# Half of a held store moved ahead of the last loads: 48 of its 128 partitions in eight transfers of 6

## The chip, the cores and the metric

The kernel runs on one core of one Trainium2 chip. The metric is the device time in microseconds of one execution: the median of 3 runs before the change is 260.25 us.

## What is computed

Attention over channels with normalised columns, then a mixture of depths in which 128 tokens of each batch pass through a small network and replace their rows. There are four batches of 6208 tokens with 256 channels, in float32.

```python
qn = q / (np.linalg.norm(q, axis=1, keepdims=True) + 1e-06)
kn = k / (np.linalg.norm(k, axis=1, keepdims=True) + 1e-06)
s = kn.transpose(0, 2, 1) @ qn / tau
a = softmax(s)                      # 256 x 256 per batch
x = v @ a                           # 6208 x 256 per batch
...
scores = np.einsum('bsd,d->bs', x, w_gate)
out = x.copy()
for b in range(B):
    top_idx = np.argpartition(-scores[b], capacity)[:capacity]
    xe = x[b, top_idx]
    ye = np.maximum(xe @ w1, 0.0) @ w2
    g = 1.0 / (1.0 + np.exp(-scores[b, top_idx]))
    out[b, top_idx] = x[b, top_idx] + g[:, None] * ye
```

## The kernel before

A batch is cut into units: six chunks of 1024 rows (128 partitions by 8 rows of 256 channels) and a remainder of 64 rows. GpSimd issues all loads, cast from float32 to bfloat16 on the way; `units` lists them batch by batch, first the q and k chunks, then the v chunks, in the order chunk 0, remainder, chunks 1 to 5. The last chunk of q and k and the last chunk of v of the last batch are loaded in two halves of four rows (`pieces`, L229).

TensorE first sums k times q over the rows of a batch. A softmax chain follows (`softmax_stages`), then the transposes of v (`p2_transpose`), the gate scores (`p2_score`) and the output products (`p2_out`), whose PSUM results ScalarE or VectorE copies into one of nine staging tiles `stage` of 128 x 8 x 256 float32 (1 MB). One staging tile is one store, issued by SyncE (`emit_store`, L671; the remainder L673). When all scores of a batch exist, `select_stages` searches the threshold of the 128 highest scores in seven steps (cmp L715, counts m_ps L735), finds the tokens (tri_b L765, oh L786), gathers their v rows (L803), transposes them (L827), runs the network and scatters the 128 updated rows (L908).

The queues are in order, and the program's order is written by a planner that runs while the kernel is built: `Engines` and `Rings` keep an estimate of each engine's and of the transfers' time, and the main loop at the end picks the piece of work whose estimated data are there. `Rings.landing` estimates when a transfer lands; `Rings.fetch` adds 1.2 us for each fetch of code to one of eight lags in turn, and a landing waits for the largest lag. Where TensorE would wait in the late phase, the planner puts in matmuls whose result nobody reads (`unread`, L593).

Stores of the last two batches, and the last two of the batch before them, are held back while loads run (`back`, `deferred`): the first of them waits for a gate (`GATE`, L230), the landing of the first half of the very last v unit, and the others stand behind it in SyncE's queue. That queue, the gate and the estimates that follow from them (`stage_ready`, `out_store`) are what the change touches.

Of the kernel before, what the change touches and what calls it, by code (L numbers as in the profile page):

```python
# [17 lines left out]
P = 128  # L18
# [11 lines left out]
class Rings:  # L30
# [9 lines left out]
        self.lag[self.fetched % 8] += FETCH  # L40
        self.fetched += 1

    def add(self, ring, ready, dur, key, tail):
        self.q[ring].append((ready, dur, key, tail))

    def run(self, until):
        while True:
            heads = [r for r in (0, 1) if self.q[r]]
            if not heads:
                return  # L50
            nxt = max(self.t, min(self.q[r][0][0] for r in heads))
            if nxt > until:
                return
            self.lag = [max(0.0, x - (nxt - self.t)) for x in self.lag]
            self.t = nxt
            able = [r for r in heads if self.q[r][0][0] <= nxt]
            r = able[0] if len(able) == 1 else 1 - self.last
            ready, dur, key, tail = self.q[r].pop(0)
            self.last = r
            self.t = nxt + dur  # L60
            self.done[key] = self.t + tail + max(self.lag)

    def landing(self, key):
        if key in self.done:
# [60 lines left out]
def kernel(  # L125
# [12 lines left out]
    nc = tc.nc  # L138
# [52 lines left out]
    def view(t, b, ci):  # L191
        if ci < NFULL:
            return lview(t, b, ci // CPL)[:, ci % CPL * RPP:(ci % CPL + 1) * RPP, :]
        return lview(t, b, NL)
# [15 lines left out]
    def late(b, ci):  # L210
        return b == E and ci in LATE

    def back(b, ci):
        return b >= E or b == E - 1 and ci in BACK

    LOAD = 2.445
    STORE = 2.45
    rings = Rings()
    eng = Engines()
# [5 lines left out]
    units = []  # L225
    for b in range(B):
        units += [("qk", b, d) for d in lorder] + [("v", b, d) for d in lorder]
    if LR == 8:
        pieces = {("qk", L, LAST): (4, 4), ("v", L, LAST): (4, 4)}  # L229
        GATE = ("v", 0) + units[-1]  # L230
    else:
        pieces = {("qk", 0, FIRST): (8, 8), ("qk", L, LAST): (8, 4, 4), ("v", L, LAST): (8, 4, 4)}
        GATE = ("v", 8) + units[-1]
    loaded = {}
    pair_of = {}
    load_inst = {}
# [127 lines left out]
    stage_of = {}  # L364
# [621 lines left out]
    def stage_ready():  # L986
# [4 lines left out]
            return stage_free[key]  # L991
        return rings.landing(("st",) + key)

    def out_store(b, ci):
        dep = stage_done[(b, ci)]
        if back(b, ci) and not gate_done:
            dep = max(dep, rings.landing(GATE))
        if late(b, ci):
            dep = max(dep, rings.landing(("scatter", E)))
        parts = (2 if b == L else 1) if ci < NFULL else 1  # L1000
        for h in range(parts):
            key = ("st", b, ci) if h == parts - 1 else ("st", b, ci, h)
            issued = eng.issue("sp", 0.42, dep)
            rings.add(1, issued + 0.65, STORE / parts + 0.009 if ci < NFULL else 0.2, key, 0.45)
            ins = emit_store(b, ci, h, parts)
        stored[b].append(key)
        if not late(b, ci):
            held[b] -= 1
        return ins

    while True:
# [17 lines left out]
        if deferred and GATE in load_inst and (held[E] == 0 or any(b == E for b, _ in deferred)):  # L1029
            for b, ci in [d for d in deferred if d[0] == E] or list(deferred):  # L1030
                deferred.remove((b, ci))
                st = out_store(b, ci)
                if not gate_done:
                    gate_done.append(1)
                    tc.add_manual_dep(
                        st.ins, load_inst[GATE].ins.name,
                        mybir.DependencyInfo(mybir.DependencyClass.Sync, mybir.DependencyReason.DATA),
                        reason="stores behind the last loads")
        t = now()
        able = []  # L1040
        for c in chains:
# [145 lines left out]
```

## Time and profile before

| | us |
|---|---|
| median of 3 runs | 260.25 |
| lowest and highest run | 258.79, 260.44 |
| the profiled execution, its own time | 259.43 |
| its span, first to last instruction | 257.4 |
| busy in the span: PE | 206.8 (80%) |
| DVE, ACT | 104.3 (41%), 99.4 (39%) |
| HBM read and written | 78.91 MB, 25.95 MB |

Times within the program count from the span's start. PE is TensorE, DVE is VectorE, ACT is ScalarE, POOL is GpSimd, SP is SyncE; SPq is SyncE's queue of transfers. DMA share is the mean busy share of the core's sixteen transfer engines, and GB/s is what they wrote, so a load counts with its bfloat16 bytes. A row of the timeline gives start, duration, engine, line, operation, output and inputs, count, and in brackets the idle time before it with what ended it.

### The profile page before, as it was taken

The page shows a single profiled execution, that of the slowest core. Times are in us where ns is not written, and L with a number is a line of the kernel's source. Part 1 is how long each engine was busy: PE and PEld are TensorE (multiplying, and loading weights), DVE is VectorE, ACT ScalarE, POOL GpSimd, SP SyncE. Part 2 cuts the span into 40 slices and gives each one's busy share as a digit, 9 for nine tenths or more (in the row PEclk, how much of TensorE's full clock was granted, in tenths as well). Part 3 has the DMA queues.
Part 4 walks back from the last instruction along what each step waited for, and adds up shares of the span by engine and source line. Part 5 has one row for each costly group of instructions (what it writes and reads, how often), then busy time and mean ns, then how long its engine had stood idle before and what let it go on. Part 6 is the DMA issues. An engine that isn't in the chain of part 4 may idle for free.

```text
span 257.4 us, 6080 instructions
## 1 busy us (share of the span) xinstructions
PE 206.8 (80%) x2585; PEld 171.4 (67%) x2585; DVE 104.3 (41%) x414; ACT 99.4 (39%) x182; POOL 56.2 (22%) x105
## 2 busy tenths in 40 slices
PE   0099697788888969999998759689998989887980
PEld 0068476676767849997676549577776879665860
DVE  0200002657552263436660011656657266676230
ACT  2800003630000587763943001660233298364750
POOL 8223223123204230100034123213214200001301
PEclk9999889799999997999999799999999999999998
DMA  6999999999999999999999999999999997999995
GB/s 236 259 218 213 213 213 211 215 212 213 213 214 212 214 259 288 279 333 313 315 291 333 308 221 211 214 212 214 211 215 212 212 211 185 402 425 414 401 419 233
DMA packets 16844, 66.84 MB, mean 260 GB/s; under 512 B 2097, under 2 KB 3634, under 8 KB 13618
## 3 DMA queue, kind: packets, MB, share of 16 engines
q0 software_dynamic: 12528, 38.93, 75.8%
q1 hardware_dynamic: 4290, 27.53, 26.4%
q8 instruction: 20, 0.33, 0.5%
q14 instruction: 6, 0.05, 0.0%
HBM read 78.91 MB, written 25.95 MB: 407 GB/s over the span
## 4 chain that ended last, share of the span: by engine, by line
DMA 54%; PE 24%; issue 8%; ACT 4%; DVE 4%; POOL 2%; POOLq 1%; SPq 0%; ACTq 0%
DMA qk_ch<-in_k_dram 29%; DMA qk_ch<-in_q_dram 13%; DMA v_ch<-in_v_dram 12%; PE o_ps L641 8%; PE s_ps L426 4%; PE g_ps L430 4%; ACT stage L659 2%; PE vt_ps L558 2%; PE m_ps L735 1%; PE sc_ps L607 1%; POOL qk_ch L261 1%; ACT vt_sb L576 1%; DVE qk_ch L579 1%; DVE cmp L715 1%; PE g_ps L641 1%
## 5 line engine op out<-in xcount | busy, mean ns | idle before, releaser
L426 PE MATMUL s_ps<-qk_ch 128*128 128x256 bf16 x288 | 68.8, 284 | 21.4 <-DMA qk_ch<-in_k_dram 21.4
L430 PE MATMUL g_ps<-qk_ch 128*128 128x256 bf16 x288 | 68.6, 284 | 0.0
L659 ACT COPY stage<-o_ps 128x512 f32<-128x512 f32 x79 | 44.7, 590 | 40.0 <-PE o_ps L641 38.0
L426 PEld LDWEIGHTS <-qk_ch 128*128 128x128 bf16 x288 | 29.3, 102 | 28.3 <-DMA qk_ch<-in_k_dram 23.3
L641 PE MATMUL o_ps<-a_sb,vt_sb 128*128 128x256 bf16 (+1 forms) x278 | 40.2, 274 | 3.1 <-ACT stage L659 2.1
L641 PEld LDWEIGHTS <-vt_sb 128*128 128x128 bf16 (+1 forms) x294 | 27.5, 98 | 9.9 <-issue 6.0
L430 PEld LDWEIGHTS <-qk_ch 128*128 128x128 bf16 x288 | 29.3, 102 | 4.5
L558 PEld LDWEIGHTS <-v_ch 128*128 128x128 bf16 x384 | 24.5, 101 | 4.2 <-issue 3.5
L558 PE MATMUL vt_ps<-ident_b,v_ch 128*128 128x128 bf16 x328 | 24.9, 226 | 2.9 <-ACT vt_sb L576 2.9
L261 POOL DMA_DIRECT2D qk_ch<-in_q_dram x25 | 13.8, 552 | 44.4 <-PE vt_ps L558 8.7
L261 POOL DMA_DIRECT2D v_ch<-in_v_dram x25 | 13.5, 551 | 29.3 <-DMA qk_ch<-in_q_dram 18.2
L466 DVE SCALAR_TENSOR_TENSOR junk<-g_ps,ident_f 128x128 f32<-128x128 f32 x6 | 1.7, 292 | 44.6 <-ACT e L457 44.5
L261 POOL DMA_DIRECT2D qk_ch<-in_k_dram x25 | 13.6, 545 | 26.7 <-DMA v_ch<-in_v_dram 15.3
L739 DVE TENSOR_REDUCE cnt<-m_ps 128x8 f32<-128x392 f32 (+2 forms) x28 | 12.0, 429 | 16.3 <-PE m_ps L735 15.9
L579 DVE COPY vt_sb<-vt_ps 128x1024 bf16<-128x1024 bf16 x20 | 13.5, 689 | 12.0 <-PE vt_ps L558 12.0
L715 DVE SCALAR_TENSOR_TENSOR cmp<-sc,wl,tab 128x392 bf16<-128x392 f32 x28 | 17.5, 627 | 1.0
L908 POOL DMA_INDIRECT out_dram<-upd,idx x4 | 4.0, 991 | 62.8 <-DMA out_dram<-stage 31.3
L576 ACT COPY vt_sb<-vt_ps 128x1024 bf16<-128x1024 bf16 (+1 forms) x19 | 16.3, 906 | 1.2 <-PE vt_ps L558 1.0
L457 ACT COPY e<-g_ps 128x256 f32<-128x256 f32 x3 | 1.1, 372 | 31.5 <-PE g_ps L430 31.5
L607 PE MATMUL sc_ps<-aw_sb,vt_sb 128*128 128x2 bf16 (+1 forms) x294 | 11.1, 164 | 1.5 <-DVE sc L683 0.6
L441 PE MATMUL s_ps<-qk_ch 128*128 128x256 bf16 x96 | 11.9, 273 | 0.0
L607 PEld LDWEIGHTS <-vt_sb 128*128 128x128 bf16 (+1 forms) x294 | 10.1, 96 | 2.7 <-DVE vt_sb L579 1.6
(180 smaller groups left out, 268.7 us busy)
## 6 DMA issues: line engine op xcount, KB each, us to landing
out_dram<-stage SPq DMA_DIRECT2D x18, 1024.0 KB, 14.3
qk_ch<-in_q_dram POOLq DMA_DIRECT2D x23, 512.0 KB, 14.6
qk_ch<-in_k_dram POOLq DMA_DIRECT2D x23, 512.0 KB, 18.9
v_ch<-in_v_dram POOLq DMA_DIRECT2D x23, 512.0 KB, 16.9
out_dram<-stage SPq DMA_DIRECT2D x12, 512.0 KB, 8.2
stage<-in_moe_w_dram SPq DMA_DIRECT2D x2, 1024.0 KB, 5.0
qk_ch<-in_q_dram POOLq DMA_DIRECT2D x2, 256.0 KB, 16.0
qk_ch<-in_k_dram POOLq DMA_DIRECT2D x2, 256.0 KB
```

What stands on the lines that cost most here:

```text
L261: ins = nc.gpsimd.dma_start(out=t[:, rows, :], in_=lview(src, b, d)[:, rows, :])
L426: nc.tensor.matmul(s_ps[:, cc, :].rearrange("p (i c) -> p i c", i=2), lhsT=pair[:parts, 1, s, cc * P:(cc + 1) * P], rhs=pair[:parts, :, s, ...
L430: nc.tensor.matmul(g_ps[:, cc, :].rearrange("p (i c) -> p i c", i=2), lhsT=blocks[:parts, at, :], rhs=blocks[:parts, at:at + step + 1:step ...
L441: nc.tensor.matmul(s_ps[:, cc, :], lhsT=kt[:parts, s, cc * P:(cc + 1) * P], rhs=qt[:parts, s, :], start=d == FIRST and s == 0 and cc == 0, ...
L558: nc.tensor.transpose(vt_ps[:, cc, j, :parts], in_=vt[:parts, v0 + j, cc * P:(cc + 1) * P], identity=ident_b[:parts, :parts])
L576: nc.scalar.copy(vt_sb[:, :, :n, :parts], vt_ps[:, :, :n, :parts])
L579: nc.vector.tensor_copy(vt_sb[:, :, :n, :parts], vt_ps[:, :, :n, :parts])
L607: nc.tensor.matmul(sc_ps[:parts, col, :], lhsT=vt_sb[:, cc, j, :parts], rhs=aw_sb[:, cc, :], start=cc == 0 and col == 0, stop=cc == 1 and ...
L641: nc.tensor.matmul(o_ps[:parts, pj, :], lhsT=vt_sb[:, cc, j, :parts], rhs=a_sb[:, cc, :], start=pj == 0 and cc == 0, stop=last and cc == 1 ...
L659: nc.scalar.copy(st[:parts, rows, :], o_ps[:parts, :m, :])
L715: nc.vector.scalar_tensor_tensor(out=cmp, in0=sc[:, :, None].to_broadcast([P, NCOL, NTHR]), scalar=wl[:, i, NTHR:NTHR + 1], in1=tab[:, Non ...
L739: nc.vector.tensor_reduce(out=cnt9[:, 0:NTHR], in_=mps[:, 0:wide * NTHR].rearrange("p (s j) -> p j s", s=wide), axis=AX.X, op=ALU.add)
```

## The change

The first held store is split. Its partitions 0 to 47 go in eight transfers of six partitions each (every fourth partition, from 0 to 3 and from 24 to 27 on); the first of the eight waits for the landing of the v unit that is fifth from the end (`EIGHTS_GATE`, chunk 1 of the last batch) and the other seven follow it in SyncE's queue. Partitions 48 to 127 go in one transfer that waits for `GATE` as the whole store did. The planner's estimates follow: each of the eight counts 0.75 us on SyncE and 0.32 us of transfer, and takes that time off the eight lags of the code fetches.

```diff
--- before.py
+++ after.py
@@ -40,8 +40,8 @@
         self.lag[self.fetched % 8] += FETCH
         self.fetched += 1
 
-    def add(self, ring, ready, dur, key, tail):
-        self.q[ring].append((ready, dur, key, tail))
+    def add(self, ring, ready, dur, key, tail, eight=False):
+        self.q[ring].append((ready, dur, key, tail, eight))
 
     def run(self, until):
         while True:
@@ -55,10 +55,12 @@
             self.t = nxt
             able = [r for r in heads if self.q[r][0][0] <= nxt]
             r = able[0] if len(able) == 1 else 1 - self.last
-            ready, dur, key, tail = self.q[r].pop(0)
+            ready, dur, key, tail, eight = self.q[r].pop(0)
             self.last = r
             self.t = nxt + dur
-            self.done[key] = self.t + tail + max(self.lag)
+            if eight:
+                self.lag = [max(0.0, x - dur) for x in self.lag]
+            self.done[key] = self.t + tail + (0.0 if eight else max(self.lag))
 
     def landing(self, key):
         if key in self.done:
@@ -228,6 +230,7 @@
     if LR == 8:
         pieces = {("qk", L, LAST): (4, 4), ("v", L, LAST): (4, 4)}
         GATE = ("v", 0) + units[-1]
+        EIGHTS_GATE = ("v", 0) + units[-5]
     else:
         pieces = {("qk", 0, FIRST): (8, 8), ("qk", L, LAST): (8, 4, 4), ("v", L, LAST): (8, 4, 4)}
         GATE = ("v", 8) + units[-1]
@@ -991,10 +994,36 @@
             return stage_free[key]
         return rings.landing(("st",) + key)
 
+    def behind(store, key):
+        tc.add_manual_dep(
+            store.ins, load_inst[key].ins.name,
+            mybir.DependencyInfo(mybir.DependencyClass.Sync, mybir.DependencyReason.DATA),
+            reason="stores behind the last loads")
+
     def out_store(b, ci):
         dep = stage_done[(b, ci)]
         if back(b, ci) and not gate_done:
+            st = stage_of[(b, ci)]
+            for i, p0 in enumerate([a + j for a in (0, 24) for j in range(4)]):
+                ps = slice(p0, p0 + 21, 4)
+                ins = nc.sync.dma_start(out=view(out, b, ci)[ps], in_=st[ps])
+                if i == 0:
+                    dep = max(dep, rings.landing(EIGHTS_GATE))
+                    behind(ins, EIGHTS_GATE)
+                issued = eng.issue("sp", 0.75, dep)
+                key = ("st", b, ci, "e", i)
+                rings.add(1, issued + 0.65, 0.32, key, 0.45, True)
+                stored[b].append(key)
             dep = max(dep, rings.landing(GATE))
+            issued = eng.issue("sp", 0.42, dep)
+            key = ("st", b, ci)
+            rings.add(1, issued + 0.65, STORE * 80 / P, key, 0.45)
+            ins = nc.sync.dma_start(out=view(out, b, ci)[48:P], in_=st[48:P])
+            behind(ins, GATE)
+            gate_done.append(1)
+            stored[b].append(key)
+            held[b] -= 1
+            return ins
         if late(b, ci):
             dep = max(dep, rings.landing(("scatter", E)))
         parts = (2 if b == L else 1) if ci < NFULL else 1
@@ -1029,13 +1058,7 @@
         if deferred and GATE in load_inst and (held[E] == 0 or any(b == E for b, _ in deferred)):
             for b, ci in [d for d in deferred if d[0] == E] or list(deferred):
                 deferred.remove((b, ci))
-                st = out_store(b, ci)
-                if not gate_done:
-                    gate_done.append(1)
-                    tc.add_manual_dep(
-                        st.ins, load_inst[GATE].ins.name,
-                        mybir.DependencyInfo(mybir.DependencyClass.Sync, mybir.DependencyReason.DATA),
-                        reason="stores behind the last loads")
+                out_store(b, ci)
         t = now()
         able = []
         for c in chains:
```

SyncE's queue round the first held store (the fourth `128x2048` of its group in before; `stage` is a staging tile, `stage_rem` that of a remainder). Before:

```order
L671 DMA out_dram<-stage 128x2048 x6
L673 DMA out_dram<-stage_rem 64x256
L671 DMA out_dram<-stage 128x2048 x4
L673 DMA out_dram<-stage_rem 64x256
L671 DMA out_dram<-stage 128x2048 x5
L671 DMA out_dram<-stage 64x2048 x2
```

After:

```order
L674 DMA out_dram<-stage 128x2048 x6
L676 DMA out_dram<-stage_rem 64x256
L674 DMA out_dram<-stage 128x2048 x3
L1009 DMA out_dram<-stage 6x2048 x8
L1021 DMA out_dram<-stage 80x2048
L676 DMA out_dram<-stage_rem 64x256
L674 DMA out_dram<-stage 128x2048 x5
L674 DMA out_dram<-stage 64x2048 x2
```

One store of 128 partitions has become eight of 6 and one of 80; all that follows stands in the order that it had.

TensorE's queue where the last v chunk is transposed (L558, L561 in after), behind fillers on `w_sb` and `ident_b`. Before:

```order
L607 MATMUL sc_ps<-aw_sb,qk_ch 128x2
L593 LDWEIGHTS ident_b
L593 MATMUL sc_ps<-w_sb,ident_b 128x256
L593 LDWEIGHTS ident_b
L593 MATMUL sc_ps<-w_sb,ident_b 128x256
L593 LDWEIGHTS ident_b
L593 MATMUL sc_ps<-w_sb,ident_b 128x256
L593 LDWEIGHTS ident_b
L593 MATMUL sc_ps<-w_sb,ident_b 128x256
L558 LDWEIGHTS v_ch
L558 MATMUL vt_ps<-ident_b,v_ch 128x128
```

After:

```order
L561 MATMUL s_ps<-ident_b,v_ch 128x128
L596 LDWEIGHTS ident_b
L596 MATMUL sc_ps<-w_sb,ident_b 128x256
L596 LDWEIGHTS ident_b
L596 MATMUL sc_ps<-w_sb,ident_b 128x256
L596 LDWEIGHTS ident_b
L596 MATMUL sc_ps<-w_sb,ident_b 128x256
L561 LDWEIGHTS v_ch
L561 MATMUL vt_ps<-ident_b,v_ch 128x128
```

Four fillers ahead of these transposes have become three. Behind them four fillers have become two, and the transposes of the chunk's first half have moved from ahead of 32 score matmuls to behind them.

TensorE's queue in the last batch's search, between the counts over partitions (`tri_b`) and the token matmuls (`oh`); each output group is four matmuls from `a_sb`. Before:

```order
L765 MATMUL m_ps<-own_b,tri_b 128x1
L641 LDWEIGHTS qk_ch
L641 MATMUL s_ps<-a_sb,qk_ch 128x256
...
L786 LDWEIGHTS oh
L786 MATMUL m_ps<-wtab,oh 128x50
```

After:

```order
L768 MATMUL m_ps<-own_b,tri_b 128x1
L644 LDWEIGHTS qk_ch
L644 MATMUL o_ps<-a_sb,qk_ch 128x256
...
L644 MATMUL g_ps<-a_sb,qk_ch 128x256
...
L789 LDWEIGHTS oh
L789 MATMUL m_ps<-wtab,oh 128x50
```

One output group (into s_ps) between the two has become two (o_ps and g_ps). Counted from the first output group of the last batch, 17 groups stood ahead of `oh` and 19 do now, so that 7 whole groups behind it have become 5; the 16 groups behind those, which also take the second-last batch's correction, are as they were. ScalarE now copies one staging piece that VectorE copied. GpSimd's queue is the same in both.

## Rows read from the trace of the kernel before

**Rows 1.** The page's slices: DMA share in tenths and GB/s, 40 slices of 6.4 us.
```profile
DMA  6999999999999999999999999999999997999995
GB/s 236 259 218 213 213 213 211 215 212 213 213 214 212 214 259 288 279 333 313 315 291 333 308 221 211 214 212 214 211 215 212 212 211 185 402 425 414 401 419 233
```

**Rows 2.** Windows by stage; the last two columns are DMA share and GB/s.
```profile
207.50:214.00 6.50, 5.59 (x88) 5.10 (x85) 3.96 (x17) 6.50 (x15) 0.00 (x0) 1.00 1.07 211
214.00:218.00 4.00, 3.85 (x78) 3.52 (x76) 2.06 (x7) 2.74 (x7) 0.00 (x0) 1.00 0.54 137
218.00:254.00 36.00, 29.20 (x342) 23.16 (x339) 17.53 (x65) 18.61 (x35) 3.95 (x4) 1.00 1.01 412
254.00:257.40 3.40, 0.00 (x0) 0.00 (x0) 0.00 (x0) 0.00 (x0) 0.00 (x0) 0.72 0.16 65
```

**Rows 3.** Windows of half a microsecond round the last load, the same columns.
```profile
214.50:215.00 0.50, 0.40 (x17) 0.31 (x13) 0.00 (x0) 0.50 (x3) 0.00 (x0) 1.00 0.53 98
215.00:215.50 0.50, 0.44 (x4) 0.31 (x4) 0.00 (x0) 0.50 (x3) 0.00 (x0) 1.00 0.64 115
215.50:216.00 0.50, 0.50 (x7) 0.41 (x6) 0.32 (x2) 0.08 (x1) 0.00 (x0) 1.00 0.61 111
216.00:216.50 0.50, 0.50 (x16) 0.50 (x14) 0.30 (x1) 0.00 (x0) 0.00 (x0) 1.00 0.35 62
216.50:217.00 0.50, 0.50 (x13) 0.50 (x11) 0.50 (x2) 0.16 (x1) 0.00 (x0) 1.00 0.06 12
217.00:217.50 0.50, 0.50 (x13) 0.50 (x11) 0.43 (x3) 0.50 (x1) 0.00 (x0) 1.00 0.05 8
217.50:218.00 0.50, 0.50 (x13) 0.50 (x11) 0.50 (x2) 0.50 (x2) 0.00 (x0) 1.00 1.23 524
```

**Rows 4.** SyncE: wait for the gate; store issues (ns min/median/max); timeline from 216 us.
```profile
SPq L671 <- DMA v_ch<-in_v_dram: 87.5, 1, 87.5
...
L671 SPq DMA_DIRECT2D out_dram<-stage x30: 332/540/1767, 90.1 to 247.8; - x30
...
216.69 0.33 SPq L671 DMA_DIRECT2D out_dram<-stage  x1
...
217.68 9.41 SPq L671 DMA_DIRECT2D out_dram<-stage  x7
```

**Rows 5.** The chain that ended last, from 204 us: start, us, what.
```profile
204.19 13.56 DMA v_ch<-in_v_dram
```

**Rows 6.** TensorE's timeline: last v transposes with fillers (L593), output groups, gathered rows (L827).
```profile
219.93 0.60 PE L593 MATMUL sc_ps<-w_sb,ident_b 128*128 128x256 bf16 x4
220.36 0.61 PE L558 MATMUL vt_ps<-ident_b,v_ch 128*128 128x128 bf16 x8
220.81 0.60 PE L593 MATMUL sc_ps<-w_sb,ident_b 128*128 128x256 bf16 x4
...
238.26 0.60 PE L641 MATMUL s_ps<-a_sb,qk_ch 128*128 128x256 bf16 x4
238.70 0.60 PE L641 MATMUL o_ps<-a_sb,qk_ch 128*128 128x256 bf16 x4
...
246.78 0.38 PE L648 MATMUL o_ps<-d_b,late_oh 128*128 128x256 bf16 x2
247.00 0.28 PE L827 MATMUL vt_ps<-ident_b,vg 128*128 128x128 bf16 x2
```

**Rows 7.** GpSimd's timeline from 236 us.
```profile
238.14 0.99 POOL L803 DMA_INDIRECT vg<-in_v_dram,idx  x1 [1.11 <-DVE idx L797]
...
251.86 0.97 POOL L908 DMA_INDIRECT out_dram<-upd,idx  x1 [7.91 <-DVE upd L894]
```

**Rows 8.** Timeline: copies into the staging tiles that waited for a store.
```profile
238.47 0.69 DVE L656 COPY stage<-o_ps 128x512 f32<-128x512 f32 x1 [0.60 <-DMA out_dram<-stage]
...
241.09 0.59 ACT L659 COPY stage<-s_ps 128x512 f32<-128x512 f32 x1 [0.29 <-DMA out_dram<-stage]
```

**Rows 9.** The page's DMA queues: the one that fetches code (packets, MB, share).
```profile
q8 instruction: 20, 0.33, 0.5%
```

## The prediction

> **What bounds the kernel now.** I read the page's slices first. DMA stands at 9 tenths from the second slice to the last but one, and dips once between, in the slice from 212 to 219 us [rows 1]. So the core is bound by its transfers, and what matters is where their engines run dry. Windows by stage say the same in numbers: a share of 1.07 while the last loads run (shares a little over 1 are overlapping packets), 0.54 for the four microseconds round the landing of the last load, 1.01 for the 36 us of stores, 0.16 in the tail [rows 2]. The hole is worth 4.00 x (1.07 - 0.54) = 2.1 us of all sixteen engines.
>
> Windows of half a microsecond show its shape [rows 3]. From 214.5 to 216.0 the share stands at 0.53 to 0.64, against 1.07 before, then it falls to 0.06: about half of the engines have finished the last loads some 2 us before the other half, and from 216.5 to the restart just before 218 nearly all are idle. The late end of the plateau is the gate. SyncE's wait for the first half of the last v unit lasted 87.5 us, the store behind it was issued at 216.69, and the first store bytes run about 1.2 us later [rows 3, 4]. The last load lands at 204.19 + 13.56 = 217.75 us [rows 5].
>
> After the hole two things run side by side. The store stream is at its full 412 GB/s until 254 [rows 2]. The compute chain of the last batch goes from the last v chunk over the threshold search and the gather (238.14) to the last scatter (251.86) [rows 7]. They are tied together: copies into the staging tiles waited for a store 0.60 us at 238.47 and 0.29 us at 241.09 [rows 8], so the matmuls whose results those copies take are already paced by when stores free tiles.
>
> **What the change does to the transfers.** It takes 48 of 128 rows of 8 KB, 393,216 bytes, out of the first held store. At 412 GB/s [rows 2] these are 0.95 us of all sixteen engines, and everything behind that store in SyncE's queue starts 0.95 us sooner, provided that the 48 rows cost the loads nothing.
>
> When they run: the gate of the eight is the landing of v chunk 1, behind which chunks 2 to 5 remain, 4 x 0.524 MB written at 211 GB/s [rows 2] = 9.9 us. The last load lands at 217.75 with one late engine, most are done by 217, so the eight are released at about 207.5. All loads have been issued by then (the last one at 204.19 [rows 5]), so nothing on GpSimd is moved. On SyncE only work waits behind them that is gated until 216.69 anyway [rows 4].
>
> Issue cost: eight more instructions. The 30 stores of before took 0.33 to 1.77 us each on SyncE, median 0.54 [rows 4]. At the median they take 4.3 us and are issued by 212; the limit is (216.69 - 207.5)/8 = 1.15 us each, above which SyncE would reach the gate late. I take the median: the long ones are in the crowded store phase. Later issues have room: seven in 9.41 us [rows 4], while 1 MB takes 2.55 us to move.
>
> What they cost the loads: nothing in before shows a six-row transfer, so this is bounded from both sides. One 8 KB row on one engine is 2.55/8 = 0.32 us (1 MB is eight such rows on each of sixteen engines). If each transfer puts one row on each of six engines, those six get 8 x 0.32 = 2.55 us more, the others none. If the six belong to the half that is done about 2 us early [rows 3], they finish at 214.5 + 2.55, about 217.05, no later than the other half and ahead of the last landing: cost 0. If they belong to the late half, the gate and the last loads come 2.55 us later. What makes one half late is the fetching of code: 20 packets that take 0.5% of sixteen engines' span [rows 9], 0.005 x 16 x 257.4 / 20 = 1.03 us each; some 17 of them fall before 215 us, and 17.5 us over eight engines are 2.2 us each, the length of the plateau. So eight engines pay for all of the code and eight for none, as the planner's own account in Rings has it, and any six of the second eight cost nothing. I take 0, at four chances in five.
>
> [...]
>
> **What it does to the order.** Two places of TensorE's queue move. The transposes of the last v chunk stand behind three filler matmuls instead of four, and two instead of four follow; in before these stand at 219.93 and 220.81 in front of the transposes and scores that feed the search [rows 6], though the chunk had landed at 217.75. Eight filler matmuls there become five, 3 x 0.11 = 0.33 us, so the search may start 0.3 us or more earlier. And 19 output groups instead of 17 stand ahead of the token matmuls on oh (L786), so two fewer (2 x 0.44 = 0.87 us [rows 6]) stand between these and the transposes of the gathered rows, which ran at 247.00 right behind the last output group [rows 6]. GpSimd's queue is unchanged. None of this can outrun the staging tiles: the copies that waited at 238.47 and 241.09 wait for stores which now land 0.95 us sooner. So the compute chain can come forward by about as much as the stores, and a little less where the gather's own landing is next: PE reached it without a wait worth a row, and it was issued 8.8 us before.
>
> **The sum.** Stores 0.95 us sooner; the scatter 0.33 to 0.95 sooner; both end together, so I take 0.85 us. The profiled execution has a span of 257.4 and took 259.43 us; it becomes 258.6. The median of the runs is 260.25, 0.8 above that execution, so I forecast 260.25 - 0.85 = 259.4 us, 0.3% less. For this kernel about 1% is what a measurement can tell from no change.
>
> **Rivals.**
>
> A, the end is held by the compute chain. From the issue of the last scatter at 251.86 to the end of the span 5.5 us pass whatever the stores do. If the gather lands no sooner (transfers behind a full queue take their turns), only the filler part is gained, 0 to 0.35 us: 260.0 us. For it: DMA is nearly empty in the tail, 0.16 [rows 2]. Against it: the copies' waits for stores [rows 8].
>
> B, the six engines are late ones, or the rows are spread over both halves. Then the gate opens up to 2.55 us later, at 219.2, and the stream of stores gains 0.95 of it back: +1.6 us, 261.85. The last landing, at 217.75 or up to 217.05 + 2.55, costs the transposes little, which stood at 220.36 anyway [rows 6]. It decides from the point at which the extra work on a late engine exceeds 0.95 us, three of eight rows. For it: no row ties the six to the early half. Against: the plateau leaves room on eight engines. [...]
>
> C, SyncE is too slow with them: at 1.77 us each they end at 207.5 + 14.2 = 221.7, the gated store starts 5.0 us late, and all stores behind it: 260.25 + 5.0 - 0.95 = 264.3. For it: the 1.77 exists [rows 4]. Against: with the engines not crowded by stores, an issue took 0.33 [rows 4].
>
> That the eight are not done before the gate, and so change nothing, needs a release after 215; the landing of chunk 1 excludes it.
>
> **Chances.** Forecast 0.60, A 0.19, B 0.15, C 0.06. More than 1% faster would need 2.6 us, more than the 2.1 us of the hole: only the scatter of runs (258.79 to 260.44) could show it, 0.02. More than 1% slower is C, and B where the late landing holds the search as well: 0.08. Within 1%: 0.90. The forecast's own range, gains of 0.4 to 1.2 us, is 259.05 to 259.85; with A at its upper end and the scatter of the runs (1.5 below the median, 0.2 above, and as much again for a median of three), the range is 258.0 to 261.2. B's full price lies outside.
>
> **What would show it.** Right: half-microsecond shares near 1 up to about 216.5 instead of the plateau; the gated store issued at 216.7 within 0.3; the last v load still landing near 217.8; copies into staging, the gather and the last scatter 0.3 to 1 us earlier. Step by step wrong: a gate issue near 219 is B; eight issues that run past 216.7 are C; everything earlier but the last scatter still at about 251.8 is A; an unchanged plateau means the six engines aren't the early ones.

## The result, and the profile after

The median is 261.69 us after the change (9 runs, 261.03 to 262.96), against 259.92 us for the kernel before on the same chip (9 runs, 258.78 to 261.12). The ratio is 1.0067, with a 95% interval of 1.0043 to 1.0090: slower by 1.7 us, not faster by 0.85. The profiled execution has a span of 260.5 us and took 262.44; it lies 0.75 above its median, that of before 0.5 below, so the two profiles stand 3.1 us apart where the medians stand 1.8.

The slices of the page, against [rows 1], show the dip before the stores where it was, and deeper (121 GB/s for 185):

```profile
DMA  6999999999999999999999999999999994999994
GB/s 234 261 216 216 211 213 215 212 213 212 214 213 216 208 264 288 267 318 316 311 303 335 316 216 213 213 211 215 215 210 211 213 222 121 391 423 414 398 424 186
```

SyncE's timeline and its waits, against [rows 4]: the eights were issued from 206.95 on, 0.74 us each, as planned. The gated store (L1021) was issued at 219.28, 2.59 us later than the 216.69 of before, after a second wait for a load of 6.3 us.

```profile
206.95 5.89 SPq L1009 DMA_DIRECT2D out_dram<-stage  x8
219.28 0.34 SPq L1021 DMA_DIRECT2D out_dram<-stage  x1
...
220.34 9.58 SPq L674 DMA_DIRECT2D out_dram<-stage  x7
...
SPq L1009 <- DMA v_ch<-in_v_dram: 76.5, 1, 76.5
...
SPq L1021 <- DMA v_ch<-in_v_dram: 6.3, 1, 6.3
```

Windows of after round the last loads, against [rows 3] (the last two columns are DMA share and GB/s). The plateau of before is filled: 0.92 where it had 0.53. But the share doesn't end there: it falls to 0.17 by 218 and stands at 0.06 to 0.07 from 218 to 220, as it stood at 0.05 to 0.06 from 216.5 to 217.5 in before. One engine of sixteen is 0.0625. So by these shares one engine alone is still loading, and the gated store waits for it. (A window counts a packet, its time and its bytes, where the packet starts, so the share of a short window can pass 1.)

```profile
214.50:215.00 0.50, 0.50 (x20) 0.50 (x18) 0.18 (x1) 0.50 (x2) 0.00 (x0) 1.00 0.92 213
...
216.00:216.50 0.50, 0.34 (x6) 0.26 (x4) 0.00 (x0) 0.50 (x3) 0.00 (x0) 1.00 0.64 152
...
217.50:218.00 0.50, 0.50 (x13) 0.50 (x11) 0.50 (x2) 0.00 (x0) 0.00 (x0) 1.00 0.17 41
218.00:218.50 0.50, 0.50 (x13) 0.50 (x11) 0.47 (x2) 0.49 (x1) 0.00 (x0) 1.00 0.07 12
...
219.50:220.00 0.50, 0.32 (x9) 0.28 (x9) 0.50 (x2) 0.43 (x1) 0.00 (x0) 1.00 0.06 12
```

The trace holds one thing more, which no view prints: the times of the sixteen increments of a load's semaphore, as many as there are engines (for each of the eights, six come as its six rows land). I read each as one engine. Those of the load that is the gate fall in groups. In before, seven come from 213.04 to 213.49, eight from 215.10 to 215.58 and one at 216.63. In after, three come by 213.18, eleven from 215.05 to 215.53, and the last two at 217.46 and 219.26. The early group has lost four of its seven: four of the six engines of the eights were early ones, and two were not.

Windows by stage, of after, against [rows 2]:

```profile
207.50:214.00 6.50, 5.59 (x75) 4.93 (x73) 4.29 (x21) 6.50 (x14) 0.00 (x0) 1.00 1.06 224
214.00:218.00 4.00, 3.84 (x86) 3.50 (x84) 1.64 (x5) 2.75 (x6) 0.00 (x0) 1.00 0.62 141
218.00:220.00 2.00, 1.80 (x41) 1.68 (x38) 1.93 (x5) 1.93 (x2) 0.00 (x0) 1.00 0.07 12
220.00:222.50 2.50, 2.47 (x47) 1.96 (x45) 1.50 (x3) 0.00 (x0) 0.00 (x0) 1.00 0.96 275
222.50:254.00 31.50, 26.00 (x274) 20.28 (x274) 14.54 (x61) 18.31 (x35) 2.98 (x3) 1.00 1.01 415
```

And of before in the same stretches:

```profile
218.00:220.00 2.00, 1.75 (x52) 1.64 (x50) 1.66 (x3) 0.77 (x1) 0.00 (x0) 1.00 0.98 393
220.00:222.50 2.50, 2.15 (x32) 1.75 (x30) 1.02 (x4) 0.00 (x0) 0.00 (x0) 1.00 1.00 380
222.50:254.00 31.50, 25.30 (x264) 19.77 (x262) 14.86 (x58) 17.84 (x34) 3.95 (x4) 1.00 1.02 416
```

Here is the second thing, which the prediction had not thought of. In the first 2.5 us of the restarted stream the engines are as busy as ever (0.96), but write 275 GB/s, where before wrote 393 at 0.98. From 222.5 on the rate is what it was.

The compute chain follows, against [rows 6, 7]: the last transposes of v stand at 221.27 (before 220.36), the gather at 239.79 (238.14), the last scatter at 254.46 (251.86). TensorE's and GpSimd's timelines of after:

```profile
221.27 0.61 PE L561 MATMUL vt_ps<-ident_b,v_ch 128*128 128x128 bf16 x8
...
239.79 0.99 POOL L806 DMA_INDIRECT vg<-in_v_dram,idx  x1 [0.30 <-issue]
...
254.46 0.97 POOL L911 DMA_INDIRECT out_dram<-upd,idx  x1 [7.81 <-issue]
```

This leaves three theories for the late gate and the loss. Late engines (rival B): at least one of the six engines was among the last with its loads, and 8 x 0.32 us came on top. Order: the moved instructions cost it. Late start: the eights run beside the last loads too late, whichever engines they use. The 275 GB/s point to a second cost, called crowding below: the rest of the store moves its rows slowly.

### The profile page after: what moved, and what is told of

The parts are those of the page before. It is cut to its first block, busy times and chain, and to the rows that moved or that the text cites. A ratio compares the mean times of both kernels' runs of the same rounds, so it can differ in the third digit from the quotient of the medians.

```text
span 260.5 us, 6083 instructions
## 1 busy us (share of the span) xinstructions
PE 210.0 (81%) x2581; PEld 174.1 (67%) x2581; DVE 103.9 (40%) x413; ACT 99.8 (38%) x183; POOL 56.2 (22%) x105
## 4 chain that ended last, share of the span: by engine, by line
PE 46%; DMA 27%; ACT 9%; issue 6%; DVE 5%; POOL 2%; POOLq 1%; SPq 0%; DVEq 0%; ACTq 0%
DMA qk_ch<-in_k_dram 11%; PE s_ps L429 8%; PE g_ps L433 8%; PE o_ps L644 7%; DMA out_dram<-stage 7%; DMA vg<-in_v_dram,idx 5%; PE vt_ps L561 5%; DMA v_ch<-in_v_dram 5%; ACT vt_sb L579 4%; PE sc_ps L610 3%; PE s_ps L444 3%; PE g_ps L414 2%; PE m_ps L738 2%; ACT stage L662 2%; ACT e L525 1%
## 5 line engine op out<-in xcount | busy, mean ns | idle before, releaser
L429 PE MATMUL s_ps<-qk_ch 128*128 128x256 bf16 x288 | 70.8, 290 | 16.1 <-DMA qk_ch<-in_k_dram 16.1
L433 PE MATMUL g_ps<-qk_ch 128*128 128x256 bf16 x288 | 70.6, 290 | 0.0
L429 PEld LDWEIGHTS <-qk_ch 128*128 128x128 bf16 x288 | 29.9, 104 | 22.4 <-DMA qk_ch<-in_k_dram 16.7
L433 PEld LDWEIGHTS <-qk_ch 128*128 128x128 bf16 x288 | 30.0, 104 | 5.3 <-issue 0.2
L561 PE MATMUL vt_ps<-ident_b,v_ch 128*128 128x128 bf16 x328 | 26.1, 232 | 3.7 <-ACT vt_sb L579 3.7
L561 PEld LDWEIGHTS <-v_ch 128*128 128x128 bf16 x384 | 25.4, 103 | 4.8 <-issue 3.5
L444 PE MATMUL s_ps<-qk_ch 128*128 128x256 bf16 x96 | 12.0, 273 | 0.0
```

Of the source, the lines that this page charges most:

```text
L429: nc.tensor.matmul(s_ps[:, cc, :].rearrange("p (i c) -> p i c", i=2), lhsT=pair[:parts, 1, s, cc * P:(cc + 1) * P], rhs=pair[:parts, :, s, ...
L433: nc.tensor.matmul(g_ps[:, cc, :].rearrange("p (i c) -> p i c", i=2), lhsT=blocks[:parts, at, :], rhs=blocks[:parts, at:at + step + 1:step ...
L444: nc.tensor.matmul(s_ps[:, cc, :], lhsT=kt[:parts, s, cc * P:(cc + 1) * P], rhs=qt[:parts, s, :], start=d == FIRST and s == 0 and cc == 0, ...
L561: nc.tensor.transpose(vt_ps[:, cc, j, :parts], in_=vt[:parts, v0 + j, cc * P:(cc + 1) * P], identity=ident_b[:parts, :parts])
```

## The experiments

In all of them the same numbers are computed and stored; only the pieces of the first held store, their gate, or the order change. A ratio is to the kernel before on the same chip.

**Order and transfers apart.** e1 has the order of the change and the store of before:

```diff
-                ins = nc.sync.dma_start(out=view(out, b, ci)[ps], in_=st[ps])
...
-            ins = nc.sync.dma_start(out=view(out, b, ci)[48:P], in_=st[48:P])
+            ins = nc.sync.dma_start(out=view(out, b, ci), in_=st)
```

> Instruction order of the changed kernel, transfers of the kernel before (one store of 128 partitions at the gate, nothing earlier). Theory 1 (a late engine: the eight transfers put 2.55 us on at least one transfer engine that is among the last to finish the loads): the gated store is issued near 216.7 us as before, time within 0.4 us of before. Theory 2 (the planner's new order costs the time): about 1.7 us slower than before, gate unchanged.

Measured: 259.74 us, ratio 0.9997 (0.9975 to 1.0020). The gated store stands where it was:

```profile
216.43 0.33 SPq L1019 DMA_DIRECT2D out_dram<-stage  x1
```

The order costs nothing that shows.

e2 has the transfers of the change, and the planner's estimates, so the order, of before:

```diff
-                issued = eng.issue("sp", 0.75, dep)
-                key = ("st", b, ci, "e", i)
-                rings.add(1, issued + 0.65, 0.32, key, 0.45, True)
...
-            rings.add(1, issued + 0.65, STORE * 80 / P, key, 0.45)
+            rings.add(1, issued + 0.65, STORE + 0.009, key, 0.45)
```

> Transfers of the changed kernel (eight of 6 partitions, then 80 at the gate), instruction order of before on all other engines. Theory 1: the gated store is issued near 219.3 us and the time is 1.4 to 2.0 us above before, as with the whole change. Theory 2: gate near 216.7, time the same as before or up to 0.9 us less.

Measured: 261.57 us, ratio 1.0073 (1.0047 to 1.0099). From the first issue of the eights to the gated store 12.33 us pass (207.93 to 220.26), as in the change (206.95 to 219.28). In the traces the compute engines' instructions stand in e1 exactly as in after, and in e2 exactly as in before. So the loss comes with the transfers.

**How many engines.** The same eight transfers, of 4 partitions (e3) and of 2 (e4), with 96 and 112 partitions at the gate. The planner, told of a larger rest, orders these two kernels a little differently from before and after; e11 below has the transfers of 2 in the order of after. The cut of e3:

```diff
-            for i, p0 in enumerate([a + j for a in (0, 24) for j in range(4)]):
-                ps = slice(p0, p0 + 21, 4)
+            for i, p0 in enumerate([a + j for a in (0, 16) for j in range(4)]):
+                ps = slice(p0, p0 + 13, 4)
```

> Eight transfers of 4 partitions (32 rows) and 96 rows at the gate. Theory 1: if the late engine is the fifth or sixth, the gate is back near 216.7 and the time 0.6 us below before (32 rows x 0.02 us); if it is among the first four, the gate stays near 219.3 and the time is up to 1.9 us above before. Theory 3 (the eight start 4.4 us after their issue and so still run beside the last loads, whichever engines they use): gate near 219.3, time 1.9 us above.

> Eight transfers of 2 partitions (16 rows) and 112 rows at the gate. Theory 1: gate near 216.7 and 0.3 us below before, unless the late engine is one of the first two; then gate near 219.3 and about 2.2 us above before. Theory 3: gate near 219.3, 2.2 us above.

Measured: e3 1.0054 (1.0027 to 1.0080), e4 1.0036 (1.0016 to 1.0057). The gated store in SyncE's timeline, e3:

```profile
217.64 0.34 SPq L1021 DMA_DIRECT2D out_dram<-stage  x1
```

and e4:

```profile
216.66 0.34 SPq L1021 DMA_DIRECT2D out_dram<-stage  x1
```

So 2 engines delay the gate by nothing (216.66 for 216.69), 4 by 0.95 us, 6 by 2.59, which is 8 rows of 0.32 us: the first two have 2.6 us or more to spare, one of the next two 1.6, and one of the last two nothing. The landings say the same: the early group of seven has five left in e4, four in e3 and three in after, so both engines of e4 were early ones, three of e3's four, and four of the six. And the packets show that each eight moves its six rows side by side: the first six of after start from 210.95 to 211.20 and take 0.32 us each. The late engines are shown. But e4 loses 0.9 us with its gate in place, and 0.32 us fewer rows to move behind it. Something else costs, and the next suspect is the rest of the store.

**The rest of the store.** e5, e6, e7 are the kernel before with its first held store cut in two, both pieces at the old gate; only the cut differs:

```diff
-            ins = emit_store(b, ci, h, parts)
+            if back(b, ci) and not gate_done:
+                cut = [nc.sync.dma_start(out=view(out, b, ci)[s], in_=stage_of[(b, ci)][s])
+                       for s in (slice(0, 48), slice(48, P))]
+                ins = cut[0]
+            else:
+                ins = emit_store(b, ci, h, parts)
```

with `slice(0, P, 2), slice(1, P, 2)` in e6 and `slice(0, 64), slice(64, P)` in e7.

> The kernel before, with its first held store cut into the two pieces of the change, partitions 0 to 47 and 48 to 127, both behind the old gate: nothing runs early, so no engine can be late because of it. Late engines alone (they explain the whole loss): the same time as before, ratio 1.000 within 0.002, since the same rows move in the same place; the restart reads a share of about 1.0 at some 400 GB/s in the 4 us behind it, as before. Theory of the rest (a store that is not of all 128 partitions moves its rows slowly, as the restart of the change showed with 300 GB/s at a full share): 10 us of packet time over 16 engines, 0.6 us, so ratio 1.002 to 1.004, and the 4 us behind the restart read under 350 GB/s at a share of 1.

> The same with the cut made otherwise: even partitions in one transfer, odd partitions in the other, so that both reach over all 128 partitions. Theory of the rest, read as crowding of partitions (what costs is which partitions the sixteen engines read at once): ratio 1.000 within 0.002 and about 400 GB/s behind the restart. Rival: the cut itself costs (two transfers instead of one, smaller ones): the same loss as with 48 and 80, 1.002 to 1.004.

> The same, cut into partitions 0 to 63 and 64 to 127: the same two sizes as even and odd, but each transfer reads only one half of the partitions. Crowding: the strongest dose, each half at up to twice the time for a row, so 1.3 to 2.5 us for the two: ratio 1.004 to 1.010, and under 300 GB/s at a share of 1 in the 4 us behind the restart. If only the number or the size of the transfers counts: as even and odd. Late engines alone: 1.000.

Measured: e5 1.0081 (1.0054 to 1.0108), e6 1.0013 (0.9993 to 1.0032), e7 1.0079 (1.0048 to 1.0109). Windows right behind the restart, of before:

```profile
217.50:219.50 2.00, 1.97 (x52) 1.85 (x49) 2.00 (x4) 1.27 (x2) 0.00 (x0) 1.00 1.08 451
```

Of e5, the same stretch:

```profile
217.50:219.50 2.00, 2.00 (x51) 1.98 (x49) 1.97 (x5) 1.62 (x2) 0.00 (x0) 1.00 1.09 184
```

Of e6, whose gate opened 0.4 us later:

```profile
218.50:219.50 1.00, 1.00 (x32) 1.00 (x30) 1.00 (x2) 0.87 (x1) 0.00 (x0) 1.00 1.09 451
```

Of e7:

```profile
218.00:220.00 2.00, 1.84 (x35) 1.53 (x33) 0.77 (x4) 0.93 (x3) 0.00 (x0) 1.00 1.01 209
```

The engines are fully busy in all four. Cut into even and odd, they write what a whole store writes; cut into halves, half as much (209 at 1.01, 451 at 1.08); cut into 48 and 80, still less. The packet of a row of 8 KB took 0.31 us on average in the windows of before and e6, 0.63 in e7 and 0.77 in e5. A cut by itself costs nothing that shows (e6, 1.0013); what costs is which partitions go together in a piece: two pieces of 64 take 0.31 us a row as even and odd and 0.63 as halves. In e5 nothing ran early, and yet it lost 2.1 us.

The whole cost can be read from one view, the queues within the window 216 to 262 us. There q1 is SyncE's queue: packets, MB, and the share of sixteen engines' 46 us that they took. Of before:

```profile
q1 hardware_dynamic: 2272, 14.81, 78.1%
```

Of after:

```profile
q1 hardware_dynamic: 2243, 14.48, 77.6%
```

Of e5:

```profile
q1 hardware_dynamic: 2288, 14.81, 81.3%
```

Of e6:

```profile
q1 hardware_dynamic: 2288, 14.81, 78.2%
```

Of e7:

```profile
q1 hardware_dynamic: 2288, 14.81, 81.9%
```

At the rate of before, the 14.48 MB of after would take 78.1 x 14.48 / 14.81 = 76.4%; they took 77.6, and 1.24% of 46 us is 0.57 us. So more than half of the 0.95 us saved was lost to slower rows. For e5 it is 3.2%, 1.47 us, for e7 1.75, for e6 0.05.

**Neighbours as a picture of the crowding.** e12 cuts the store into eight transfers of 16 partitions, each eight apart:

```diff
-                       for s in (slice(0, 64), slice(64, P))]
+                       for s in [slice(a, P, 8) for a in range(8)]]
```

> The kernel before with its first held store cut into eight transfers of 16 partitions, every eighth partition each (0, 8, ..., 120, then 1, 9, ..., 121, and so on), all behind the old gate. [...] Neighbouring partitions or addresses (a row is slow when rows close to it, in the stage or in DRAM, are moved at the same time): the sixteen rows of each transfer lie as far apart as those of the full store, so rows take the usual 0.31 us, the work of SyncE's queue behind 216 stays at 78.1% of the window 216 to 262 within 0.4. [...]

Measured: 263.72 us, ratio 1.0133 (1.0079 to 1.0186), and the work of SyncE's queue, its share in the view of the queues, 81.0%, where neighbours as the cause had forecast 78.1. A window of e12 behind the restart:

```profile
218.00:219.00 1.00, 1.00 (x26) 1.00 (x24) 1.00 (x3) 1.00 (x2) 0.00 (x0) 1.00 0.99 262
```

Two transfers of 16 rows start in this microsecond (262 GB/s), and a row takes 0.49 us: not the 0.63 of the halves, but well above 0.31, though no two rows of a transfer are neighbours, neither in the stage nor in DRAM. So closeness isn't it. SyncE's eight issues took 5.85 us besides; they are the likely rest of the loss, beyond the 1.33 us of work.

Behind the restart even and odd wrote 451 GB/s (e6), the transfers of 16 rows 262, the halves 209 (e7), 48 and 80 only 184 (e5), all at a share of 0.99 to 1.09. The rests of e3 (96 partitions), e4 (112) and e14 below (120) are crowded too, by 0.42, 0.46 and 1.85 us. Which rows the engines read at the same moment no run shows, so why some cuts are crowded stays open.

**Late start, or late engines.** e10 releases the eights 10.5 us earlier; order and transfers are those of the change:

```diff
+        EIGHTS_LOAD = ("k", 0) + units[-9]
...
-                    behind(ins, EIGHTS_GATE)
+                    behind(ins, EIGHTS_LOAD)
```

> The change, with the eights released some 10 us earlier (at a chunk of k that lands near 198 instead of the v chunk that lands near 207); order and transfers are those of the change. Late engines: the six engines have the same 8 rows more to move before they are done with the loads, whenever these come, so the gated store stays near 219.3 and the ratio at 1.005 to 1.008. Rival, the eights come too late to be done in time and only their tail holds the gate: the gate goes back to 216.7 to 217.3 and the ratio falls to 1.002 or less (the crowding of the rest stays).

Measured: 261.28 us, ratio 1.0062 (1.0040 to 1.0085). SyncE's timeline:

```profile
196.41 5.89 SPq L1010 DMA_DIRECT2D out_dram<-stage  x8
219.07 0.34 SPq L1022 DMA_DIRECT2D out_dram<-stage  x1
```

The last row of the eights starts at 206.52, some 10 us ahead of the old gate, and yet the gate doesn't come back (219.07). The late start falls: rows that come 10.5 us earlier delay the gate by 2.38 us, those of the change by 2.59.

**Clean pieces.** e9 sends the even partitions early, in one transfer in place of the eight, and the odd ones at the gate:

```diff
-                ps = slice(p0, p0 + 21, 4)
+                ps = slice(0, P, 2)
...
-            ins = nc.sync.dma_start(out=view(out, b, ci)[48:P], in_=st[48:P])
+            ins = nc.sync.dma_start(out=view(out, b, ci)[1:P:2], in_=st[1:P:2])
```

> The change, with other pieces: the even partitions (64 rows) go early in one transfer at the gate of the eights, the odd partitions at the old gate. Each of the sixteen engines takes 4 rows early, 4 x 0.32 = 1.28 us, the late ones too, and both pieces reach over all 128 partitions. Late engines with crowding: the gated store is issued 1.28 us later than the 216.7 of before, near 217.9, the store behind the gate is 1.28 us shorter, nothing is crowded: ratio 1.000 within 0.002. If rows placed early cost the loads nothing as long as they are not crowded: gate at 216.7 and ratio 0.995 to 0.997. If something else in an early store costs: 1.004 or more.

Measured: 260.03 us, ratio 1.0010 (0.9988 to 1.0031), gated store 1.13 us late. Its line and its row of the queues:

```profile
217.82 0.48 SPq L1021 DMA_DIRECT2D out_dram<-stage  x1
...
q1 hardware_dynamic: 2208, 14.29, 75.4%
```

14.29 MB at the rate of before are 75.4%: nothing is crowded. Half a store (the 48 partitions of the change are three eighths) moved ahead of the gate delays the gate by about what it saves, 1.13 for 1.28 us, and no gain is left. That is the best version with an early part among these runs; none beats the kernel before.

e8 keeps the eights and makes the rest clean: the eights take even partitions, the rest goes as the 64 odd ones and the last 16 even ones.

```diff
-                ps = slice(p0, p0 + 21, 4)
+                ps = slice(2 * i, 2 * i + 81, 16)
...
+            ins = nc.sync.dma_start(out=view(out, b, ci)[1:P:2], in_=st[1:P:2])
...
+            nc.sync.dma_start(out=view(out, b, ci)[96:P:2], in_=st[96:P:2])
```

> The change, with the same 8 transfers of 6 partitions at the same gate, but taken from the even partitions 0 to 94, so that the rest is one transfer of the 64 odd partitions and one of the 16 even partitions 96 to 126. Late engines: the gated store is still issued near 219.3, 2.6 us late, since the engines of the eights are the same. Crowding of the rest: most of its 0.6 us goes, the 4 us behind the restart read 370 GB/s or more, and the ratio falls from the 1.0067 of the change to 1.003 to 1.005. If crowding is nothing: 1.006 to 1.008.

Measured: 1.0066 (1.0035 to 1.0097). The gate was at 219.35 as expected and the crowding fell from 0.57 to 0.17 us, but the time didn't fall. SyncE needed 2.65 us from the gated store to the first full store (219.35 to 222.00; after 1.06), and the share drops to 0.62 and 0.53 in the two half microseconds from 222 on: the small pieces moved faster than SyncE issued them. The interval is too wide to say more.

e11 does the same with the transfers of 2: `slice(2 * i, 2 * i + 17, 16)`, then `[1:P:2]` and `[32:P:2]`.

> The transfers of 2 again (e4, whose gate was where that of before is), taken from the even partitions 0 to 30; the rest goes as the 64 odd partitions and the 48 even ones from 32 on. Crowding as the cause of e4's 0.9 us: most of it goes, 0.32 us of rows is saved on all engines, and up to 0.3 us of crowding stays in the piece of 48: ratio 0.998 to 1.001. If the 0.9 us of e4 had another cause (eight more transfers, their semaphores, the order): 1.003 to 1.004 again.

Measured: 1.0032 (1.0010 to 1.0053), a miss: crowding fell from 0.46 to 0.27 us and the loss remained.

**The end of the span.** What e4 and e11 lose besides is seen at the other end. From the last window of 0.1 us in which the kernel's data move (code fetches left out) to the end of the span, 1.6 to 1.9 us pass in before (255.6 to 257.4), e1, e5, e6, e7, e9 and e12, and 2.2 to 2.3 us in after (258.2 to 260.5), e2, e3, e4, e8, e10 and e11. The second group has eight narrow transfers, and it also has 45 or 46 transfers on SyncE where the others have 37 to 44. e13 cuts the first eight full stores, far ahead of the last loads, into even and odd, which makes 45 without a narrow one; e14 takes four early transfers of 2 partitions, 41 in all.

```diff
+            if parts == 1 and ci < NFULL and len(cut) < 8:
+                cut.append(1)
+                emit_store(b, ci, 0, 2)
+                ins = emit_store(b, ci, 1, 2)
+            else:
                 ins = emit_store(b, ci, h, parts)
```

> The kernel before, with its first eight full stores (all far ahead of the last loads) each cut into even and odd partitions, so that SyncE issues as many transfers as in the change (eight more than before), all over sixteen engines and all 128 partitions; nothing else is touched. If the number of SyncE's instructions makes the end longer: from the last bytes moved to the end of the span about 2.0 us instead of 1.5, and a ratio of 1.001 to 1.003. If it is the narrow transfers: 1.5 us, and 1.000 within 0.002.

```diff
-            for i, p0 in enumerate([a + j for a in (0, 24) for j in range(4)]):
-                ps = slice(p0, p0 + 21, 4)
+            for i, p0 in enumerate(range(4)):
+                ps = slice(p0, p0 + 5, 4)
...
-            ins = nc.sync.dma_start(out=view(out, b, ci)[48:P], in_=st[48:P])
+            ins = nc.sync.dma_start(out=view(out, b, ci)[8:P], in_=st[8:P])
```

> The change with four early transfers of 2 partitions (0 to 7) instead of eight of 6, and the other 120 partitions at the old gate: narrow transfers, but only four issues more than before. Narrow transfers as the cause of the longer end: about 2.0 us from the last bytes moved to the end of the span. The number of SyncE's instructions: about 1.5 us. The gate stays where it was (216.4 to 217.0, as in e4). [...]

Measured: e13 1.0030 (0.9991 to 1.0069), e14 1.0071 (1.0040 to 1.0102). The last such window of e13, whose span is 258.0:

```profile
255.60:255.70 0.10, 0.00 (x0) 0.00 (x0) 0.00 (x0) 0.00 (x0) 0.00 (x0) 1.00 0.03 0
```

That is 2.3 us without a narrow transfer; in e14 it is 1.8 (258.2 to 260.0) with four of them. So the number of SyncE's instructions goes with the half microsecond, and the narrowness doesn't. The trace of SyncE's instructions shows the place: the second group has 83 or 84 of them, and in each run the 80th starts 0.45 or 0.46 us after the end of the 79th, where the instructions of that place in before follow in 0.04 or 0.05. The first group has 74 to 79 and no such gap there; e12, with 81, has it (0.47), but the wait ahead of its last instruction is 0.15 us instead of the 0.46 of the others, which hides most of it. In the second group a fetch of 8 KB of code falls into the span's end as well, 0.6 to 0.9 us behind that instruction; in the first it comes after the span. The queues of after from 259 us to the end:

```profile
q14 instruction: 1, 0.01, 1.3%
```

So SyncE stops for 0.45 to 0.47 us at the same place of its code, ahead of the 80th instruction, which only the longer programs reach. The fetch that is seen comes too late to be what it waits for there; that stays open.

**The terms together**, in us against before: the shift of the gated store, the rows that no longer stand behind it (2.55 x partitions / 128), the crowding from the queues' view, the end (against 1.8), their sum, the span of the same execution (against 257.4), and the measured difference of the medians (259.9 x (ratio - 1), with its interval).

| | gate | rows | crowding | end | sum | span | measured |
|---|---|---|---|---|---|---|---|
| after | 2.59 | -0.95 | 0.57 | 0.5 | 2.7 | 3.1 | 1.7 (1.1 to 2.3) |
| e10 | 2.38 | -0.95 | 0.58 | 0.4 | 2.4 | 3.0 | 1.6 (1.0 to 2.2) |
| e3 | 0.95 | -0.64 | 0.42 | 0.5 | 1.2 | 1.3 | 1.4 (0.7 to 2.1) |
| e4 | 0.0 | -0.32 | 0.46 | 0.5 | 0.6 | 0.9 | 0.9 (0.4 to 1.5) |
| e11 | -0.25 | -0.32 | 0.27 | 0.5 | 0.2 | 0.7 | 0.8 (0.3 to 1.4) |
| e9 | 1.13 | -1.28 | 0.0 | -0.2 | -0.3 | 0.1 | 0.3 (-0.3 to 0.8) |
| e5 | 0.09 | 0 | 1.47 | -0.1 | 1.5 | 2.3 | 2.1 (1.4 to 2.8) |
| e6 | 0.36 | 0 | 0.05 | -0.1 | 0.3 | 0.7 | 0.3 (-0.2 to 0.8) |
| e7 | 0.27 | 0 | 1.75 | -0.1 | 1.9 | 2.6 | 2.0 (1.2 to 2.8) |
| e14 | 0.10 | -0.16 | 1.85 | 0.0 | 1.8 | 2.6 | 1.8 (1.0 to 2.7) |

The terms come from one execution each, so the sum is to be held against the span beside it. It lies 0.1 to 0.8 us below in every row: either the terms leave something out, or the one execution of before was a quick one. The medians are another matter, since two executions of a kernel differ by up to 2.3 us (before, 258.78 to 261.12). After and e10 lose 0.8 to 1.0 us less than their sum by the medians, but in the executions that the terms come from they lost more than it, 3.1 and 3.0 us; so this is no sign that a late gate isn't passed on in full. e2 is left out (its execution was 1.0 us late already where the eights were issued), as are e8 and e12, where SyncE's issues weigh, and e13, told at the end.

## Why the prediction was wrong

**The step that failed first** is "What they cost the loads", and in it the sentence that eight engines pay for all of the code and eight for none, so that "any six of the second eight cost nothing. I take 0". The plateau [rows 3] did show that about half of the engines had 2 us to spare; nothing showed that the six were among them, and the four chances in five had no row behind them but a planner's account. By the landings seven engines were early, not eight, and only four of the six were among them; that code fetches make the others late, no run shows. The term was 2.59 us instead of 0: the full 8 x 0.32 that the prediction itself gives for a late engine. e3, e4 and e10 show it.

**The second** is "everything behind that store in SyncE's queue starts 0.95 us sooner": the price of a row was taken from whole stores and used for a piece of 80 partitions. The rows left cost 0.57 us more; the term is 0.4, not 0.95, and e5 loses 1.47 us in this way with nothing moved early. Rival B took the same 0.95. No row of before had the price of a block of partitions: the stores that it cuts in two are cut into every second one (L671).

**The third** was in no sum: 0.5 us at the end of the span with eight more instructions on SyncE.

**Rival B** had the mechanism, the place (a gate near 219.2; it was 219.28) and, with 261.85 for 261.69, the time. The time fits better than its sum deserves: B had 2.55 - 0.95, while the runs show two more costs, and with them the table comes to 2.7. That the medians stand at 1.7 is in part luck. Its chance of 0.15 was the error, and so the range, which ended at 261.2, left it out.

**Right**: the release (207.5 forecast, 206.95 in the profile), and the room for SyncE's issues (0.74 us each, more than the 0.54 taken and less than the limit of 1.15; rival C didn't happen). The plateau was filled, as said. The moved order costs nothing that shows (e1); that it would bring 0.3 us or more was neither seen nor excluded, as e1's interval reaches 0.6 us either way. Rival A, the compute chain holding the end, wasn't put to the test, since the stores came no sooner.

## What to carry to other kernels

An average share of 0.5 in a hole says how many engines are idle, not which; work put on a few engines is free only if these are the idle ones. Here the two of e4 were (gate at 216.66 for 216.69), while two of the six were not, and the gate came 2.59 us late. The increments of a load's semaphore, one by one, tell how many engines are early (seven here), and so does a trial with fewer rows (e3, e4). If a store must be cut, the cut into even and odd is the one that cost nothing that shows here (e6: 0.31 us a row, ratio 1.0013), while every block of partitions tried (0.63 us a row in e7, 0.77 in e5) and partitions eight apart (0.49 in e12) moved slowly. Read GB/s beside the share: full share at half the rate (209 GB/s at 1.01 in e7, 451 at 1.08 in before) is crowding. Where small pieces moved faster than SyncE issued them, the engines ran dry (0.62 and 0.53 in e8).

## What was not expected of the hardware

The store of 120 partitions in e14 cost more than the one of 128 in before: the work of e14 is 81.8% for 14.75 MB, 1.85 us above the rate of before. No run shows why. In e5, too, the piece of 48 and that of 80 behind it wrote 184 GB/s, less than the 209 of the halves.

The landing that gates the stores moves by itself. In e13, whose stores were only cut far ahead of the loads, the gated store was issued 1.2 us sooner than in before:

```profile
215.52 0.33 SPq L671 DMA_DIRECT2D out_dram<-stage  x1
```

Yet the last bytes moved at 255.7 us (before 255.6). By the terms of the table it should have gained 0.8 us, and it lost 0.8 (-0.2 to 1.8). The increments tell why the gate moved: in before one engine came 1.05 us behind the other fifteen (216.63), and a fetch of 16 KB of code, 0.89 us long, had started at 214.41; in e13 the last two came together at 215.47, and the fetch started at 216.18, behind the gate. The late engine shows at the second half of that load instead, where its last increment comes at 218.26 (before 217.74). So the last engine was done later, not sooner, while the gate opened earlier. This speaks for the last engine rather than the gate as what sets the end; one run doesn't prove it, and that the fetch delays that engine is an inference from when it starts.
